# Start-up of a channel attention and gated feed-forward kernel: squares in PSUM, sums on two engines, eight units scored from high and low parts

## The chip, the cores and the metric

The kernel runs on one core of a Trainium2 chip. The metric is the device time of one execution in microseconds (us); before the change it is 2156.61 us, the median of three runs (2156.08 to 2156.77).

## What is computed

Four batches of q, k and v, each of 6080 rows and 256 channels in float32, go through an attention over channels, and its output through a feed-forward layer with the gate g = h * sigmoid(1.702 h):

```python
qn = q / (norm(q, axis=1) + 1e-6)
kn = k / (norm(k, axis=1) + 1e-6)
s = kn.T @ qn / tau            # 256 x 256 per batch
a = softmax(s - s.max(-1))     # divided by the sum + 1e-9
x = v @ a                      # 6080 x 256
h = x @ w_in                   # 256 -> 2048
out = (h * sigmoid(1.702 * h)) @ w_out
```

## The kernel before, in words

The rows of a batch lie on 128 partitions. Each partition holds 47 rows, and a tail of 64 rows is left. The work is cut into 25 units: units 0 to 22 have two row groups each (tiles of 128 x 512), units 23 and 24 have one (128 x 256). For one unit the scores take four products, of a 128 x 128 slice of k with 256 columns of q, in float32. The trace records each such float32 product as two matmuls (L348).

The first batch stands alone at the start, since nothing is there to overlap it with. `start_up` (L832) writes its order out by hand:

- SyncE loads q and k in tiles of up to six row groups, in order, into buffers of their own (L265, L269). GpSimd clears two tails (L268).
- For each unit, `prepare` (L279) squares q and k on ScalarE (L292) into one of three SBUF buffers. VectorE adds the two squares together, 1024 columns at once (L295), into one of two running sums. Even units go to one sum and odd units to the other.
- `score` (L365) of unit u - 7 is put behind `prepare` of unit u, on TensorE's queue. The scores collect in PSUM bank "o3". The first 18 units' scores are issued here, those of units 18 to 24 by the planner below.
- After the loads of the first batch, SyncE loads the first weights: `win_fetch` (L158, DMA at L120) into the buffers "qs" and "ks" of the pool `sp`, then `wout_fetch`, tau, `v_load` and the next batch's first rows.
- `add_both` (L298) adds the two sums and then the two halves (L300, L301). That finishes the sums of squares, called "acc" by the planner.

`first_softmax` (L852) and `together` (L1109) then lay out everything from the scores of unit 18 to the end of the first eight pairs of feed-forward blocks. They make a list of nodes with an engine, a duration and what they depend on. `arrange` (L1010) places them along a modelled time. The order on TensorE is fixed, except for the next batch's first scores, which are flexible fill. It is: scores of units 18, 19 and 20, the norms (`first_norms`, L449, matmul L453), scores 21 and 22, the spread of the norms (L480), scores 23 and 24, then the transposes of the softmax (L524). The model takes the time at which this stretch begins from START, that of the sums from `late_at(40.2, "acc")` (L869), and the first free times of ScalarE and VectorE from L1015. From the norms on, ScalarE takes their root (L460), VectorE turns it (L467 to L471), ScalarE makes a diagonal (L476), and so on to the softmax, while both engines also convert weights and split v.

After that the pairs follow (`lay`, L1537). There TensorE has matmuls of 512 columns on operands that are split into a high part (rounded to float32r) and a low part (the rest), with three products each. VectorE makes the low parts (L784 in the feed-forward, L312 for the scores of later batches) and GpSimd adds the squares of later batches (L332) and sums of v (L686).

The buffers that the change touches: the pool `sp` gives "qs" and "ks" two buffers each, the pool `vp` gives "pz_h" and "pz_l" two each. A buffer is given out again when its last reader is done. PSUM has eight banks of 512 float32: "a", "b", "c", "s" and "o0" to "o3".

Of the kernel before, what the change touches and what calls it, by code (L numbers as in the profile page):

```python
# [2 lines left out]

# [1 line left out]

# [6 lines left out]
F32 = mybir.dt.float32  # L12
F32R = mybir.dt.float32r
U32 = mybir.dt.uint32
AF = mybir.ActivationFunctionType
ALU = mybir.AluOpType
# [3 lines left out]
P = 128  # L20
# [3 lines left out]
NCH = 512  # L24
# [4 lines left out]
def channel_attention_then_glu(  # L29
# [23 lines left out]
    nc = tc.nc  # L53
    B, N, C = q.shape
# [7 lines left out]
    T = N // P  # L62
    TAIL = N - T * P
    UT = 2
    RT = 2
    SLOTS = 4
    WCH = 2 * NCH
    NCHUNK = -(-N // WCH)
    short = [NCHUNK - 2 if 0 < b < B - 1 else NCHUNK - 1 for b in range(B)]
    widths = [[WCH] * n + [N - (NCHUNK - 1) * WCH] + [WCH] * (NCHUNK - 1 - n) for n in short]  # L70
    chunks = [[(sum(w[:c]), w[c]) for c in range(NCHUNK)] for w in widths]
    STEPS = NF // 2 * SLOTS

    const = ctx.enter_context(tc.tile_pool(name="const", bufs=1))
    wp = ctx.enter_context(tc.tile_pool(name="wp", bufs=1))
    vp = ctx.enter_context(tc.tile_pool(name="vp", bufs=1))
    gp = ctx.enter_context(tc.tile_pool(name="gp", bufs=1))
    op = ctx.enter_context(tc.tile_pool(name="op", bufs=3))
    sp = ctx.enter_context(tc.tile_pool(name="sp", bufs=2))
    dram = ctx.enter_context(tc.tile_pool(name="dram", bufs=1, space=bass.MemoryType.DRAM))  # L80
    cv = ctx.enter_context(tc.tile_pool(name="cv", bufs=2))
# [5 lines left out]
    def bank(tag, name):  # L87
        pool = {"a": ps_h, "b": ps_h, "c": ps_h, "s": ps_s}.get(tag, ps_o)
        return pool.tile([P, NCH], F32, tag=tag, name=name)
# [65 lines left out]
    words = {}  # L155
    win = {}

    def win_fetch(n):  # L158


        g, c = divmod(n, NC2)
        gs = slice(2 * g * GW, 2 * (g + 1) * GW)
        src = w_in[c * P : (c + 1) * P, gs].rearrange("p (f w) -> p f w", w=2)
        if g == 0:
            room = (sp, ("qs", "ks")[c])
        else:
            room = (wp, f"{('wh', 'wl')[c]}{g}")
        words["in", n] = load_words(src, [P, GW], *room)
# [6 lines left out]
    def wout_fetch(u):  # L175

        rows = w_out[2 * u * P : 2 * (u + 1) * P, :]
        src = rows.rearrange("(f p) (d w) -> p f d w", p=P, w=2)
        words["out", u] = load_words(src, [P, 2, C])
# [19 lines left out]
    class Attention:  # L199
# [31 lines left out]

        def rooms(self, t0, room):
            n = (t0 + 4) // 6
            if t0 in (T - 3, T - 1):
                n = (t0 - T + 3) // 2
                tiles = [gp.tile([P, NCH], F32, tag=f"{t}{n}", name="raw") for t in ("gh", "gl")]
                return [t.rearrange("p (u c) -> p u c", u=UT) for t in tiles]
            if n in (4, 5):
                t = wp.tile([P, 2, NF // 2, C], F32, tag=("wo_h", "wo_l")[n - 4], name="raw")
                return [t[:, i] for i in range(2)]  # L240
            return [
                wp.tile([P, 6, C], F32, tag=f"{t}{n % 6}", name=f"raw_{s}")
                for t, s in (("wh", "q"), ("wl", "k"))
            ]

        def load(self, t0, room):

            b = self.b
            nt = min(room, T - t0)

            early = self.early.pop(0) if self.early else None
            cuts = (0, nt)
            if self.alone:
                tiles = self.rooms(t0, room)
                cuts = {2: (0, 2, 4, 6), 8: (0, 2, 6)}.get(t0, cuts)
            elif early:
                tiles = [
                    vp.tile([P, room, C], F32, tag=early + t, name="raw", bufs=2) for t in ("_h", "_l")
                ]
            else:  # L260
                tiles = [sp.tile([P, RT, C], F32, tag=t, name=t) for t in ("raw_q", "raw_k")]
            for a, z in zip(cuts, cuts[1:]):
                for src, t in zip((q, k), tiles):
                    body = src[b, : T * P, :].rearrange("(p t) c -> p t c", p=P)
                    nc.sync.dma_start(t[:, a:z, :], body[:, t0 + a : t0 + z, :])  # L265
                    if z == nt < room and TAIL:

                        nc.gpsimd.memset(t[TAIL:, nt, :], 0.0)  # L268
                        nc.sync.dma_start(t[:TAIL, nt, :], src[b, T * P :, :])  # L269
            for o in range(room):  # L270
                self.raw[t0 + o] = [t[:, o:, :] for t in tiles]
# [7 lines left out]
        def prepare(self, u):  # L279
            nt = self.units[u][1]  # L280
            if u == 0:
                self.sums_both = both = cv.tile([P, 2, UT, C], F32, tag="words", name="sums")
                *self.squares, self.sums_odd = [
                    vp.tile([P, 2, UT, C], F32, tag=tag, name="squares", bufs=2)
                    for tag in ("px_h", "px_l", "py_h", "py_l")
                ]
            elif u == 1:
                both = self.sums_odd
            else:
                both = self.squares[u % 3]  # L290
            for n, r in enumerate(self.fetched(u)):
                nc.scalar.activation(both[:, n, :nt, :], r, AF.Square)  # L292
            if u > 1:
                acc = (self.sums_both, self.sums_odd)[u % 2][:, :, :nt, :]
                nc.vector.tensor_tensor(acc, acc, both[:, :, :nt, :], op=ALU.add)  # L295
            return self.fetched(u)

        def add_both(self):  # L298
            acc = self.sums_both
            nc.vector.tensor_tensor(acc, acc, self.sums_odd, op=ALU.add)  # L300
            nc.vector.tensor_tensor(acc[:, :, 0, :], acc[:, :, 0, :], acc[:, :, 1, :], op=ALU.add)  # L301

        def part(self, u, n):
            nt = self.units[u][1]
            tag = ("qs", "ks")[n]
            self.parts[u, n] = t = sp.tile([P, UT, 2, C], F32R, tag=tag, name=tag)
            nc.scalar.copy(t[:, :nt, 0, :], self.fetched(u)[n])
# [57 lines left out]
        def score(self, u, qs, ks):  # L365
            nt = self.units[u][1]
            if u == 0:
                self.start_scores("o3")
            steps = [(j, i) for j in range(nt) for i in range(NC2)]
            last = u == len(self.units) - 1  # L370
            for j, i in steps:
                self.product(i, ks[:, j, i * P : (i + 1) * P], qs[:, j, :], last and j == nt - 1)

        def score_half(self, u):

# [440 lines left out]
    def keep_warm():  # L816

        wide = gp.tile([P, NCH], F32, tag="g", name="wide", bufs=2)
        nc.vector.memset(wide, 1.0)
        ps = bank("b", "ps_y")  # L820
        for rhs in [ones] * 4 + [wide]:
            nc.tensor.matmul(ps[:, : rhs.shape[1]], lhsT=ones, rhs=rhs, start=True, stop=True)  # L822

    nu = len(range(0, T, UT)) + (TAIL > 0)
    ats = [Attention(b, nu if b == 0 else 4 if b == 1 else 0) for b in range(B)]
    at, nxt = ats[:2]
# [5 lines left out]
    def start_up():  # L832
        nc.scalar.activation(table, ones[:, 0:1], AF.Sqrt)
        keep_warm()
        for u in range(nu):
            ready.append(at.prepare(u))
            if u >= AHEAD:
                at.score(u - AHEAD, *ready[u - AHEAD])
        win_fetch(0)
        win_fetch(1)  # L840
        wout_fetch(0)
        nc.sync.dma_start(tau_sb, tau.partition_broadcast(P))
        v_load(0, 0, False)
        v_load(0, 0, True)
        nxt.fetched(0)
        nxt.fetched(2)
        win_fetch(2)
        win_fetch(3)
        at.add_both()
        wo.extend(wp.tile([P, NF, C], F32R, tag=f"wo_{n}", name=f"wo_{n}") for n in "hl")  # L850

    def first_softmax():  # L852

        A = at
        us = 1.0 / 0.68
        START = 36.4

        def add(eng, dur, token, deps, fn, *a):
            gather[0].append(Node(eng, dur * us, token, deps, fn, a))

        def score(u, *deps):
            dur = 0.86 if u == nu - 1 else 1.72
            add("PE", dur, ("s", u), deps, lambda: at.score(u, *ready[u]))

        def late_at(t, *tokens):
            for token in tokens:
                done(token, (t - START) * us)

        late_at(40.2, "acc")  # L869
        late_at(34.7, ("cv", "in", 0, "load"))  # L870
        late_at(36.0, ("cv", "in", 1, "load"))
        late_at(37.3, ("cv", "out", 0, "load"))
# [137 lines left out]
    def arrange(nodes, row, ahead, near):  # L1010
# [1 line left out]
        ends = dict(begun_ends)  # L1012
        row = list(row)
        clock = dict.fromkeys(("PE", "ACT", "POOL", "SP"), 0.0)
        clock["ACT"], clock["DVE"] = 3.0, 5.6  # L1015
        open_to = {e: [] for e in clock}
        users = {}
        unmet = {}
# [39 lines left out]
        while undone:  # L1058
            best = None
            for e in clock:  # L1060
                at = list(choices(e))
                if not at:
                    continue
                t = min(r for r, _ in at)
# [13 lines left out]
            if best is None:  # L1078
                r, x = min((c for e in clock for c in choices(e)), key=lambda c: c[0])
                best = r, r, x  # L1080
            _, t, x = best
# [582 lines left out]
    for b in range(B):  # L1664
        for c in range(NCHUNK):
            if b or c:
                p = (b * NCHUNK + c) * PAIRS
                v_job(b, c, p - 1, p - 5)
        if b + 1 < B:
            o = b * NCHUNK * PAIRS  # L1670
            u, last_u = ats[b + 1].direct, len(ats[b + 1].units)
# [16 lines left out]
    with tc.manual_schedule():  # L1688
        start_up()
        together(PAIRS)  # L1690
        for p in range(PAIRS, TOTAL):
# [3 lines left out]
            t = now[0]  # L1695
# [33 lines left out]
```

## Time and profile before

| | |
|---|---|
| median of 3 runs | 2156.61 us |
| profiled execution: its own time | 2157.14 us |
| profiled execution: span from first to last instruction | 2155.4 us |
| TensorE busy | 2148.2 us |
| ScalarE busy | 1551.9 us |
| VectorE busy | 1288.2 us |
| GpSimd busy | 431.2 us |
| chain that ended last | TensorE 99% |

The profile is of one execution, whose own time is 0.5 us above the median. A timeline row gives the start, the duration, the engine (PE is TensorE, PEld its weight loads, DVE is VectorE, ACT is ScalarE, POOL is GpSimd, SPq the queue of SyncE), the source line, the operation, what is written from what is read, and the count. Instructions of one engine overlap a little at their ends, so the pace of a queue is the distance between starts, which is somewhat less than a duration.

### The profile page before, as it was taken

To read this page: it belongs to the slowest core of one execution; us is meant where nothing else is said; L and a number is where in the kernel's file an instruction comes from. 1 tells how busy PE (TensorE), PEld (TensorE's weight loads), DVE (VectorE), ACT (ScalarE), POOL (GpSimd) and SP (SyncE) were. 2 spreads that over 40 slices of the span, in tenths; PEclk is the share of its full clock that TensorE was granted. 3 is DMA by queue.
4 is the path that set the end of the run, shared out by engine and by line. 5 is a ranking of instruction groups with operands and counts; after the bars stand their busy time and mean duration, and the time that the engine had idled before them with its cause. 6 is when DMAs were issued, how large, how long until landed. Compare 5 with 4: busy or idle time off the path is not lost.

```text
span 2155.4 us, 26555 instructions
## 1 busy us (share of the span) xinstructions
PE 2148.2 (100%) x9720; PEld 1794.0 (83%) x9720; DVE 1288.2 (60%) x1925; ACT 1551.9 (72%) x2753; POOL 431.2 (20%) x457
## 2 busy tenths in 40 slices
PE   9999999999999999999999999999999999999999
PEld 8888888888888888888888888888888888888887
DVE  7986656665556665664555666566555545545543
ACT  7987777766777777776777777777676666666665
POOL 0003333230113342231012233223111200100100
PEclk9999999999999999999999999999999999999999
DMA  9433222221122222221113222122111110110100
GB/s 373 142 104 97 69 68 78 68 71 40 59 97 67 62 88 59 73 79 40 39 61 106 69 69 74 54 87 66 40 67 50 59 40 20 59 40 20 57 20 19
DMA packets 73843, 153.50 MB, mean 71 GB/s; under 512 B 6896, under 2 KB 14576, under 8 KB 73712
## 3 DMA queue, kind: packets, MB, share of 16 engines
q1 hardware_dynamic: 73712, 151.81, 21.3%
q8 instruction: 76, 1.25, 0.2%
q14 instruction: 55, 0.45, 0.1%
HBM read 122.68 MB, written 29.10 MB: 70 GB/s over the span
## 4 chain that ended last, share of the span: by engine, by line
PE 99%; ACT 1%; DMA 0%; issue 0%; DVE 0%; SPq 0%; ACTq 0%
PE ps_o L797 48%; PE ps_x L721 24%; PE ps_z L721 12%; PE ps_y L721 6%; PE s L387 4%; PE s L348 2%; PE ps_w L586 2%; PE ps_w L604 0%; DMA words<-in_w_in 0%; PE ps_y L822 0%; ACT vh L705 0%; PE ps_n L414 0%; ACT wf L621 0%; ACT eighths L136 0%; ACT z L134 0%
## 5 line engine op out<-in xcount | busy, mean ns | idle before, releaser
L797 PE MATMUL ps_o<-gh,wo_l 128*128 128x512 f32 (+1 forms) x1536 | 594.9, 387 | 0.0
L797 PE MATMUL ps_o<-gh,wo_h 128*128 128x512 f32 (+1 forms) x1536 | 594.8, 387 | 0.0
L797 PE MATMUL ps_o<-gl,wo_h 128*128 128x512 f32 (+1 forms) x1536 | 470.6, 387 | 0.0
L784 DVE TENSOR_TENSOR gl<-g,gh 128x512 fp32r<-128x512 f32 (+1 forms) x384 | 275.4, 756 | 155.7 <-ACT gh L780 155.7
L332 POOL TENSOR_TENSOR acc<-acc,sq 128x256 f32<-128x256 f32 x276 | 217.2, 793 | 600.5 <-ACT sq L320 589.7
L797 PEld LDWEIGHTS ps_o<-gh,wo_h 128*128 128x128 f32 x1536 | 288.3, 188 | 57.6
L797 PEld LDWEIGHTS ps_o<-gl,wo_h 128*128 128x128 f32 x1536 | 288.3, 188 | 57.5
L797 PEld LDWEIGHTS ps_o<-gh,wo_l 128*128 128x128 f32 x1536 | 288.3, 188 | 57.3
L784 DVE TENSOR_TENSOR gl<-ps_y,gh 128x512 fp32r<-128x512 f32 (+1 forms) x192 | 131.7, 686 | 339.0 <-ACT gh L780 338.6
L721 PE MATMUL ps_x<-vh,wh 128*128 128x512 f32 (+1 forms) x768 | 299.6, 390 | 0.6 <-ACT g L775 0.2
L721 PE MATMUL ps_x<-vl,wh 128*128 128x512 f32 (+1 forms) x768 | 298.0, 388 | 0.0
L721 PE MATMUL ps_x<-vh,wl 128*128 128x512 f32 (+1 forms) x768 | 297.5, 387 | 0.0
L686 POOL TENSOR_TENSOR v_raw<-v_raw 128x512 f32<-128x512 f32 (+1 forms) x110 | 167.8, 1534 | 515.6 <-DMA v_raw<-in_vT 433.7
L775 ACT ACTIVATE r<-r 128x512 f32<-128x512 f32 (+1 forms) x192 | 120.5, 628 | 170.1 <-DVE r L764 170.1
L755 ACT COPY r<-ps_x 128x512 f32<-128x512 f32 (+1 forms) x189 | 110.1, 583 | 168.8 <-PE ps_x L721 168.4
L780 ACT CAST gh<-g 128x512 fp32r<-128x512 f32 (+1 forms) x384 | 216.4, 613 | 0.1
L784 DVE TENSOR_TENSOR gl<-r,gh 128x512 fp32r<-128x512 f32 (+1 forms) x192 | 149.8, 780 | 61.6 <-ACT gh L780 58.4
L721 PEld LDWEIGHTS ps_x<-vh,wh 128*128 128x128 f32 x768 | 144.4, 188 | 29.3 <-ACT g L775 1.6
L721 PEld LDWEIGHTS ps_x<-vh,wl 128*128 128x128 f32 x768 | 144.2, 188 | 29.0
L721 PEld LDWEIGHTS ps_x<-vl,wh 128*128 128x128 f32 x768 | 144.5, 188 | 25.3
L755 ACT COPY r<-ps_z 128x512 f32<-128x512 f32 (+1 forms) x192 | 111.9, 583 | 71.6 <-PE ps_z L721 70.5
L405 DVE TENSOR_TENSOR sums<-sums,s 128x256 f32<-128x256 f32 x138 | 58.0, 420 | 160.2 <-PE s L387 157.8
(137 smaller groups left out, 3274.7 us busy)
## 6 DMA issues: line engine op xcount, KB each, us to landing
v_raw<-in_vT SPq DMA_DIRECT2D x80, 512.0 KB, 4.3
out_T<-osb SPq DMA_DIRECT2D x80, 256.0 KB, 2.0
raw_q<-in_q SPq DMA_DIRECT2D x74, 256.0 KB, 2.7
raw_k<-in_k SPq DMA_DIRECT2D x74, 256.0 KB, 2.7
win_h<-win_h SPq DMA_DIRECT2D x16, 512.0 KB, 3.3
win_l<-win_l SPq DMA_DIRECT2D x16, 512.0 KB, 4.2
v_raw<-in_vT SPq DMA_DIRECT2D x16, 480.0 KB, 3.8
words<-in_w_in SPq DMA_DIRECT2D x8, 512.0 KB, 5.2
```

The lines of the kernel that those rows point to most:

```text
L332: nc.gpsimd.tensor_tensor(acc, acc, sq[:, j, :], op=ALU.add)
L348: nc.tensor.matmul(self.s[:, i, :], lhsT=lhsT, rhs=rhs, start=self.first, stop=last, skip_group_check=True,)
L387: nc.tensor.matmul(out, lhsT=ks[:, j, low, ci], rhs=rhs, start=n == 0, stop=n == len(terms) - 1, skip_group_check=True,)
L405: nc.vector.tensor_tensor(out, out, part, op=ALU.add)
L586: nc.tensor.matmul(ps, lhsT=l[:, j, ci], rhs=r[:, j, :], start=n == 0, stop=n == 3 * NC2 - 1,)
L686: eng.tensor_tensor(out, a, z, op=ALU.subtract)
L721: nc.tensor.matmul(out, lhsT=l[:, wi, :], rhs=r[:, n, : self.hw], start=first and m == 0, stop=last and m == 2, skip_group_check=True,)
L755: nc.scalar.copy(r, getattr(self, src))
L775: nc.scalar.activation(g, source, AF.Gelu_apprx_sigmoid)
L780: nc.scalar.copy(gh, g)
L784: nc.vector.tensor_tensor(gl, g, gh.bitcast(F32), op=ALU.subtract)
L797: nc.tensor.matmul(out[d][:, : self.hw], lhsT=l[:, at_f, d * P : (d + 1) * P], rhs=r, start=first and l is wo[0] and r is gh, stop=last an ...
```

## The change

Squares of the first batch are written to six PSUM banks in turn, one for q and one for k of a unit, and VectorE adds each of them to a single running sum, 512 columns at a time. Units 4, 7, 10, 13 and 16 are left out of that: their squares go to SBUF, and GpSimd adds them to a second sum, which unit 1 began. VectorE joins the two sums behind unit 20's adds and folds the halves behind unit 22's. For units 6, 8, 10, ... 20 a new function, `split_unit`, copies q and k to their rounded high parts on ScalarE and subtracts these on VectorE for the low parts, just ahead of `prepare` of the unit after next. TensorE then scores such a unit by three products in place of one (high-high, high-low, low-high). The clearing of the tails goes from GpSimd to VectorE at the very start. The planner's figures are set anew.

```diff
+    LAST_ODD = 16
+    SPLIT = tuple(range(6, 21, 2))
...
         def prepare(self, u):
             nt = self.units[u][1]
             if u == 0:
...
+                self.rooms_ps = cycle(("a", "c", "o0", "o1", "o2", "b"))
+            odd = u % 3 == 1 and u <= LAST_ODD
+            acc = (self.sums_both, self.sums_odd)[odd]
             for n, r in enumerate(self.fetched(u)):
-                nc.scalar.activation(both[:, n, :nt, :], r, AF.Square)
-            if u > 1:
-                acc = (self.sums_both, self.sums_odd)[u % 2][:, :, :nt, :]
-                nc.vector.tensor_tensor(acc, acc, both[:, :, :nt, :], op=ALU.add)
+                if u < 2:
+                    out = acc[:, n]
+                elif odd:
+                    out = self.squares[u // 3 % 3][:, n]
+                else:
+                    out = bank(next(self.rooms_ps), "sq").rearrange("p (u c) -> p u c", u=UT)
+                out = out[:, :nt, :]
+                nc.scalar.activation(out, r, AF.Square)
+                if u > 1:
+                    eng = nc.gpsimd if odd else nc.vector
+                    eng.tensor_tensor(acc[:, n, :nt, :], acc[:, n, :nt, :], out, op=ALU.add)
             return self.fetched(u)

-        def add_both(self):
+        def add_odd(self):
             acc = self.sums_both
             nc.vector.tensor_tensor(acc, acc, self.sums_odd, op=ALU.add)
+
+        def add_halves(self):
+            acc = self.sums_both
             nc.vector.tensor_tensor(acc[:, :, 0, :], acc[:, :, 0, :], acc[:, :, 1, :], op=ALU.add)
+
+        def split_unit(self, u):
+            m = SPLIT.index(u)
+            for n, r in enumerate(self.fetched(u)):
+                pool, tag = (sp, ("qs", "ks")[n]) if m % 3 else (vp, ("pz_h", "pz_l")[n])
+                self.parts[u, n] = t = pool.tile([P, UT, 2, C], F32R, tag=tag, name=("qs", "ks")[n])
+                nc.scalar.copy(t[:, :, 0, :], r)
+                nc.vector.tensor_tensor(t[:, :, 1, :], r, t[:, :, 0, :].bitcast(F32), op=ALU.subtract)
...
             for j, i in steps:
-                self.product(i, ks[:, j, i * P : (i + 1) * P], qs[:, j, :], last and j == nt - 1)
+                ci = slice(i * P, (i + 1) * P)
+                if self.alone and u in SPLIT:
+                    qp, kp = self.parts[u, 0], self.parts[u, 1]
+                    for l, r in ((0, 0), (0, 1), (1, 0)):
+                        self.product(i, kp[:, j, l, ci], qp[:, j, r, :])
+                else:
+                    self.product(i, ks[:, j, ci], qs[:, j, :], last and j == nt - 1)
...
     def start_up():
...
+        at.tail_room()
         for u in range(nu):
+            if u - 2 in SPLIT:
+                at.split_unit(u - 2)
             ready.append(at.prepare(u))
+            if u == LAST_ODD + 4:
+                at.add_odd()
+            elif u == nu - 3:
+                at.add_halves()
             if u >= AHEAD:
                 at.score(u - AHEAD, *ready[u - AHEAD])
...
-        at.add_both()
...
+    START, ACC = 34.7, 39.2
...
-        START = 36.4
...
-            dur = 0.86 if u == nu - 1 else 1.72
+            dur = 0.86 if u >= nu - 2 else 1.44 if u in SPLIT else 1.72
...
-        late_at(40.2, "acc")
+        late_at(ACC, "acc")
...
-        clock["ACT"], clock["DVE"] = 3.0, 5.6
+        clock["ACT"], clock["DVE"] = (38.0 - START) / 0.68, (ACC - START) / 0.68
```

## Rows read from the trace of the kernel before

**Rows 1.** Busy time by stretch: us, PE, PEld, DVE, ACT, POOL, granted clock, DMA.

```profile
17.60:38.00 20.40, 20.40 (x96) 17.97 (x95) 18.41 (x16) 17.55 (x35) 0.00 (x0) 1.00 1.00 396
...
41.40:70.00 28.60, 26.95 (x130) 20.93 (x129) 28.27 (x65) 25.18 (x51) 0.00 (x0) 1.00 0.80 300
70.00:131.00 61.00, 61.00 (x302) 50.92 (x301) 60.10 (x123) 56.88 (x112) 0.00 (x0) 1.00 0.33 113
131.00:200.00 69.00, 68.70 (x305) 55.96 (x304) 45.50 (x68) 53.78 (x96) 14.68 (x18) 1.00 0.28 88
```

**Rows 2.** The chain that ended last, at the start-up: start, us, what.

```profile
6.92 34.77 PE s L348 x160
41.70 0.87 PE ps_n L453 x8
```

**Rows 3.** Timeline of PE: six products with split operands, and what follows them.

```profile
55.39 0.40 PE L604 MATMUL ps_w<-win_h,aT_h 128*128 128x256 f32 x2
55.63 0.40 PE L604 MATMUL ps_w<-win_l,aT_h 128*128 128x256 f32 x2
...
56.84 2.75 PE L348 MATMUL s<-raw 128*128 128x256 f32 x12
```

**Rows 4.** Timeline of ACT: squares of units 7 and 8, and the last ones.

```profile
17.14 0.63 ACT L292 ACTIVATE squares<-raw_k 128x512 f32<-128x512 f32 x1 [1.22 <-DMA raw_k<-in_k]
17.67 0.62 ACT L292 ACTIVATE squares<-raw_q 128x512 f32<-128x512 f32 x1
18.19 0.61 ACT L292 ACTIVATE squares<-raw_k 128x512 f32<-128x512 f32 x1
...
35.53 2.36 ACT L292 ACTIVATE squares<-raw 128x512 f32<-128x512 f32 x6
```

**Rows 5.** Timeline of DVE: sums of squares from unit 7 on, and what follows.

```profile
17.80 1.23 DVE L295 TENSOR_TENSOR squares<-squares 128x1024 f32<-128x1024 f32 x1 [1.31 <-ACT squares L292]
...
36.99 1.22 DVE L295 TENSOR_TENSOR sums<-sums,squares 128x1024 f32<-128x1024 f32 x1
38.13 0.68 DVE L295 TENSOR_TENSOR squares<-squares 128x512 f32<-128x512 f32 x1
38.73 0.68 DVE L295 TENSOR_TENSOR sums<-sums,squares 128x512 f32<-128x512 f32 x1
39.45 1.23 DVE L300 TENSOR_TENSOR sums<-sums,squares 128x1024 f32<-128x1024 f32 x1
40.71 0.69 DVE L301 TENSOR_TENSOR sums<-sums 128x512 f32<-128x512 f32 x1
...
45.08 0.14 DVE L467 RECIPROCAL rtau<-tau_sb 128x1 f32<-128x1 f32 x1
```

**Rows 6.** One line's instructions each: duration ns min/median/max, first and last start.

```profile
L760 ACT COPY ps_y<-ps_x x192: 543/570/607, 61.4 to 2137.6; 128x512 f32<-128x512 f32 x160, 128x480 f32<-128x480 f32 x32
...
L784 DVE TENSOR_TENSOR gl<-g,gh x384: 648/687/1789, 70.8 to 2146.4; 128x512 fp32r<-128x512 f32 x160, 128x480 fp32r<-128x480 f32 x32
...
L784 DVE TENSOR_TENSOR gl<-ps_y,gh x192: 648/692/693, 65.3 to 2141.4; 128x512 fp32r<-128x512 f32 x160, 128x480 fp32r<-128x480 f32 x32
...
L686 POOL TENSOR_TENSOR v_raw<-v_raw x110: 1212/1620/1787, 174.2 to 2045.7; 128x512 f32<-128x512 f32 x90, 128x480 f32<-128x480 f32 x20
```

**Rows 7.** Timelines of DVE and POOL where both work, around 200 us.

```profile
201.08 1.11 DVE L312 TENSOR_TENSOR ks<-raw_k,ks 128x512 fp32r<-128x512 f32 x1
215.25 2.55 DVE L784 TENSOR_TENSOR gl<-g,gh 128x512 fp32r<-128x512 f32 x2 [0.86 <-ACT gh L780]
237.06 1.30 DVE L784 TENSOR_TENSOR gl<-g,gh 128x512 fp32r<-128x512 f32 x2 [1.12 <-ACT gh L780]
...
200.07 1.56 POOL L332 TENSOR_TENSOR acc<-acc,sq 128x256 f32<-128x256 f32 x2 [2.19 <-ACT sq L320]
214.12 4.83 POOL L686 TENSOR_TENSOR v_raw<-v_raw 128x512 f32<-128x512 f32 x3 [0.87 <-DMA v_raw<-in_vT]
```

**Rows 8.** Timelines of SyncE and ACT: first weights issued, first wait for v.

```profile
30.98 2.20 SPq L120 DMA_DIRECT2D words<-in_w_in  x2
...
42.61 1.14 ACT L705 CAST vh<-v_raw 128x512 fp32r<-128x512 f32 x2 [2.00 <-DMA v_raw<-in_vT]
```

More of the change, by code (lines that the diff above doesn't have):

```diff
@@ L1 @@
 from contextlib import ExitStack
-from itertools import product
+from itertools import cycle, product
 import numpy as np
@@ L233, in rooms @@
             n = (t0 + 4) // 6
-            if t0 in (T - 3, T - 1):
+            if t0 == T - 1:
+                return self.tail
+            if t0 == T - 3:
                 n = (t0 - T + 3) // 2
@@ L244, in rooms, with tail_room @@
             ]
+        def tail_room(self):
+            tiles = [gp.tile([P, NCH], F32, tag=t, name="raw") for t in ("gh1", "gl1")]
+            self.tail = [t.rearrange("p (u c) -> p u c", u=UT) for t in tiles]
+            for t in self.tail:
+                nc.vector.memset(t[TAIL:, 1, :], 0.0)
         def load(self, t0, room):
@@ L266, in load @@
                     if z == nt < room and TAIL:
-                        nc.gpsimd.memset(t[TAIL:, nt, :], 0.0)
+                        if not self.alone:
+                            nc.gpsimd.memset(t[TAIL:, nt, :], 0.0)
                         nc.sync.dma_start(t[:TAIL, nt, :], src[b, T * P :, :])
@@ L281, in prepare @@
             if u == 0:
-                self.sums_both = both = cv.tile([P, 2, UT, C], F32, tag="words", name="sums")
+                self.sums_both = cv.tile([P, 2, UT, C], F32, tag="words", name="sums")
                 *self.squares, self.sums_odd = [
@@ L286, in prepare @@
                 ]
[L287 to L290, printed above, removed]
+                self.rooms_ps = cycle(("a", "c", "o0", "o1", "o2", "b"))
+            odd = u % 3 == 1 and u <= LAST_ODD
+            acc = (self.sums_both, self.sums_odd)[odd]
             for n, r in enumerate(self.fetched(u)):
-                nc.scalar.activation(both[:, n, :nt, :], r, AF.Square)
-            if u > 1:
-                acc = (self.sums_both, self.sums_odd)[u % 2][:, :, :nt, :]
-                nc.vector.tensor_tensor(acc, acc, both[:, :, :nt, :], op=ALU.add)
+                if u < 2:
[9 more added lines that the diff above has]
+                    eng.tensor_tensor(acc[:, n, :nt, :], acc[:, n, :nt, :], out, op=ALU.add)
             return self.fetched(u)
-        def add_both(self):
+        def add_odd(self):
             acc = self.sums_both
             nc.vector.tensor_tensor(acc, acc, self.sums_odd, op=ALU.add)
+        def add_halves(self):
+            acc = self.sums_both
             nc.vector.tensor_tensor(acc[:, :, 0, :], acc[:, :, 0, :], acc[:, :, 1, :], op=ALU.add)
+        def split_unit(self, u):
[5 more added lines that the diff above has]
+                nc.vector.tensor_tensor(t[:, :, 1, :], r, t[:, :, 0, :].bitcast(F32), op=ALU.subtract)
         def part(self, u, n):
```

## The prediction

> **What bounds the kernel now.** I read the busy times by stretch first, then the chain of waits, then each engine's timeline up to 60 us. From 70 us on TensorE is never idle and nothing there is edited, so only the start-up can move the time, and any delay made there stays [rows 1]. Up to 41.7 us the chain is TensorE alone: 160 matmuls of scores, units 1 to 20, without a gap, then the norms [rows 2]. One float32 record takes 34.77 / 160 = 0.217 us, a unit of eight 1.74 us. So unit 6 starts at 6.92 + 5 x 1.74 = 15.6 and unit 20 ends at 41.7. The other thing to see is how little room the neighbours have. ScalarE's last squares end at 37.9 [rows 4]; the sums of squares are done at 40.71 + 0.69 = 41.4 [rows 5], 0.3 us before the norms want them. From 41.4 to 131 us VectorE is busy for 88.4 of 89.6 us [rows 1], so it cannot catch up there.
>
> **TensorE's saving.** Twelve 256-column products with split operands take 56.84 - 55.39 = 1.45 us, weight loads included [rows 3]; a split unit needs just twelve. That is 0.29 less than 1.74, and 2.3 us for eight units, if operands are on time.
>
> **The first operands are late.** The copies of unit 6 are issued ahead of unit 8's squares, so behind unit 7's. The latter waits for its k until 17.14 [rows 4]; the pace of ScalarE is 18.19 - 17.67 = 0.52. So the copies start at 17.67 and 18.19, the second ends at 18.8, and VectorE's second subtraction (0.68) at 19.6. Now TensorE starts unit 6 at 15.6: it will stand still for about 4.0 us. That is more than the 2.3 saved. The loads that set 17.14 are not edited.
>
> **ScalarE.** Left from 17.67 on: 30 squares of 512 columns (units 8 to 22) at 0.52 = 15.6, four half squares at (2.36 - 2 x 0.52) / 4 = 0.33 [rows 4] = 1.3, and 16 copies at 0.52 = 8.3. Sum 25.2, so 42.9 where it was 37.9. No row has a square into PSUM; a copy from PSUM to PSUM has 0.57 for 0.62 [rows 4, 6], which would take 1.2 off for 24 squares, and I take the SBUF row, nothing else being known. Copies and squares cannot be hidden behind loads any more: after 17.6 ScalarE was busy for 17.6 of 20.4 us [rows 1], 2.8 free for 8.3.
>
> **VectorE.** Its pace is 1.14 for 1024 columns (38.13 - 36.99) and 0.60 for 512 (38.73 - 38.13) [rows 5]. From 18.3 on it has 24 adds of 512 (the twelve units from 8 to 22 that GpSimd does not take) = 14.4, 16 subtractions = 9.6, four adds of 256 at about 0.33 (0.60 less 256 columns at 0.54 per 512) = 1.3, the joining 1.14 and the folding 0.60. Sum 27.0, end 45.3. Some 1 us more goes where it waits for ScalarE, which has four operations where a split unit gives VectorE two: 46.4. An add from PSUM has a duration of 0.69 at most [rows 6], like one from SBUF; were 0.69 its pace too, 24 would cost 2.2 more, and I keep 0.60 as duration and form agree. GpSimd takes only four units off this stretch (7, 10, 13, 16), 4.6 us, while the splits bring 9.6. So without any clash the sums are ready at 46.4, 5.0 late.
>
> **The clash with GpSimd.** Ten adds of 512 on GpSimd at 1.2 to 1.8 us [rows 6] fill some 15 us of 11 to 33. In the rows where both work, a VectorE subtraction with two SBUF operands that starts at 201.08, in the middle of GpSimd's pair (200.07 to 201.63), takes 1.11 for 0.69, and ends 0.56 after the pair; two at 215.25 take 2.55, where the same two alone take 1.30 [rows 7]. The form with one PSUM operand never exceeds 693 ns, the one with two SBUF operands reaches 1789 [rows 6]. The squares in PSUM dodge this; the 16 subtractions do not. Those of units 8 to 16 fall among the adds of 10, 13 and 16. A pair that meets them costs 0.4 (one rest) to about 2 (a rest and a whole add), 1.25 in the row. Five pairs: 2 to 10, or nothing if they slip between. I take four at 1.25 = 5, as the row of the pair is the nearest. With them the sums come at 51.4, 10.0 late. The Trainium skill (SBUF — State Buffer, Who interferes with whom) has the same rule: a VectorE instruction with two SBUF inputs and a GpSimd one that reads SBUF exclude each other for a whole instruction. By it this trace's 1.11 and 2.55 are no accident, and a clash-free start-up should not be expected.
>
> **What waits behind.** With three units' banks in turn, ScalarE's square waits for VectorE's add of three units back, so ScalarE is held at VectorE's pace, at no extra cost. The buffers "qs" and "ks" have two rooms each; `win_fetch(0)` gets that of unit 16, so SyncE's load, issued at 30.98 [rows 8], now waits for score 16, near 43 in my sum, and tau, v and the next batch's rows queue behind it. The loads before it have drained by then, and the engines that want these words are as late, so I cost it at nothing; the cover is gone if SyncE is released later than 8 us ahead of the first use of v (42.61 before [rows 8]). add_odd's wait for GpSimd ends long before unit 20. Moved clearings of the tails: two short writes in an empty queue, nothing.
>
> **Sum.** Norms at 51.5 for 41.7: 9.8 late. VectorE continues its solid stretch 10 late. What can be given back is idle time of before: 1.65 us on TensorE and 0.33 on VectorE from 41.4 to 70, 0.9 on VectorE to 131 [rows 1]. I take 1.0. Delay 8.8. The profiled execution, 2157.14, would become 2165.9; the median lies 0.5 below it: 2165.4.
>
> **Rivals.**
> No clash: the subtractions slip between GpSimd's adds. Norms 4.8 late, less 1.0: 2160.4. For it: ScalarE feeds VectorE slowly and unevenly; against it, rows 7.
> Only the first stall: adds and copies are quicker than their rows and catch up by unit 20. 4.0 - 2.3 = 1.7 late: 2158.3. Against it, 27.0 us of work from 18.3 on.
> The other side: operands and sums are on time, and TensorE's saving decides: 2.3 less, 2154.3. It decides where unit 6's low part is there by 15.6 and the sums by 41.7 - 2.3 = 39.4. For it: TensorE is the only engine in the chain today. Against it: k of unit 7 lands at 17.1 and is ahead in ScalarE's queue.
> The clock: TensorE's granted clock is 1.00, the 2.4 GHz level, in all stretches [rows 1], where it hardly stood idle; idle times of 4 us at unit 6 and shorter ones after it are new. At 1.2 GHz a product takes twice as long. Up to the norms that is mostly hidden behind VectorE; if the clock is still low then, scores 21 to 24 (three units' work, 5.2 us) take 5 more: 2170.4. No row here shows the clock fall. The Trainium skill (TensorE: Matmul & The Clock Gate, the section on the HAM clock gate) says that idle time brings the half rate.
>
> **Numbers.** Forecast 0.60 (own range 2162 to 2170, clash 2 to 10 less what is given back), no clash 0.20, only the first stall 0.07, the gain 0.04, the clock 0.09. A measurement can tell about 0.2%, 4.3 us: the bounds are 2152.3 and 2160.9. Faster 0.02, as TensorE's whole saving falls short of 4.3. Same 0.19: the first stall, the rest of the gain and nearly half of no clash. Slower 0.79. The range 2159 to 2170.5 holds the forecast and no clash and leaves out the lowest two and the clock's upper end.
>
> **What would show it.** In the profile after: TensorE idle for some 4 us before unit 6 and again before later even units; VectorE solid from 18 to 50 us, its subtractions of units 8 to 16 at 1 to 2 us where GpSimd is busy, its adds from PSUM at 0.69; ScalarE's last squares near 47; the first w_in load issued after 37; norms near 51; the first 512-column matmuls of the pairs 9 us later than now. I am wrong if unit 6 starts before 17, or the norms before 45, or if the delay at the norms is gone by 131 us.

## The result and the profile after

The changed kernel takes 2169.72 us (median of six runs, 2169.11 to 2170.68) against 2156.69 for the kernel before, run beside it: 13.0 us more, a ratio of 1.006 with a 95% interval of 1.0047 to 1.0073. That is inside the predicted range and 4.3 above the predicted value. The profiled execution, whose own time of 2170.59 is 0.9 above the median, has a span of 2168.7 for 2155.4. Two executions of the record, one of the kernel before and one of the run without splits, took 3081 us at a mean granted clock of 0.65 and count in no median or ratio below.

TensorE's timeline shows most of it at a glance; the last bracket is the idle time ahead of an instruction and what ended it.

```profile
4.62 11.46 PE L376 MATMUL s<-raw_q,raw_k 128*128 128x256 f32 x48
18.93 0.39 PE L376 MATMUL s<-qs,ks 128*128 128x256 f32 x1 [2.85 <-ACT ks L328]
19.86 3.11 PE L376 MATMUL s<-qs,ks 128*128 128x256 f32 x11 [0.54 <-DVE qs L329]
...
26.23 1.46 PE L376 MATMUL s<-qs,ks 128*128 128x256 f32 x10 [1.02 <-DVE ks L329]
...
40.36 1.78 PE L376 MATMUL s<-qs,ks 128*128 128x256 f32 x12
...
43.51 1.78 PE L376 MATMUL s<-qs,ks 128*128 128x256 f32 x12
...
48.03 0.38 PE L376 MATMUL s<-qs,ks 128*128 128x256 f32 x1 [0.89 <-DVE qs L329]
48.63 1.45 PE L376 MATMUL s<-qs,ks 128*128 128x256 f32 x10 [0.22 <-DVE ks L329]
51.74 1.87 PE L487 MATMUL ps_n<-ones,sums 128*128 128x1 f32 x8 [1.65 <-DVE sums L312]
53.47 3.76 PE L376 MATMUL s<-raw_q,raw_k 128*128 128x256 f32 x8
57.02 2.15 PE L376 MATMUL s<-raw 128*128 128x256 f32 x8
```

The six units up to 16.08 run without a gap, as before. Unit 6 then waits 2.85 us for its high parts and 0.54 more for a low part. The later waits are for VectorE's low parts (ks, qs, L329) and at 51.74 for its sums. The same place in the trace of before, from the norms to unit 22:

```profile
41.55 1.02 PE L453 MATMUL ps_n<-ones,sums 128*128 128x1 f32 x8
42.43 1.97 PE L348 MATMUL s<-raw_q,raw_k 128*128 128x256 f32 x8
44.24 1.89 PE L348 MATMUL s<-raw 128*128 128x256 f32 x8
```

The norms come 10.0 us later than the 41.70 of [rows 2], or 10.2 from start to start in the two timelines. Then something else shows: the norms take 1.87 for 1.02, and unit 21's eight records 57.02 - 53.47 = 3.55 for 44.24 - 42.43 = 1.81. From the start of the norms to that of unit 22 it is 5.28 for 2.69, 2.6 us more. The busy times by stretch, TensorE alone, give the reason in the column of the granted clock (us, busy, clock, DMA share, GB/s):

```profile
18.00:20.00 2.00, 0.52 (x2) 0.99 1.01 421
20.00:22.00 2.00, 1.89 (x8) 0.50 1.04 433
...
50.00:52.00 2.00, 0.35 (x3) 0.68 0.92 343
52.00:54.00 2.00, 2.00 (x9) 0.50 1.06 411
54.00:56.00 2.00, 2.00 (x6) 0.50 1.05 416
56.00:58.00 2.00, 2.00 (x7) 0.62 1.02 411
```

After the waits ahead of unit 6, and from within the wait ahead of the norms, the clock is at 0.50, the 1.2 GHz level. The trace of before has 1.00 in every stretch of [rows 1].

VectorE's timeline, to be read beside [rows 5]: subtractions are L329 and adds L312. GpSimd's adds are the POOL rows of the second listing.

```profile
18.39 1.42 DVE L329 TENSOR_TENSOR qs<-raw_q,qs 128x512 fp32r<-128x512 f32 x1 [2.28 <-ACT qs L328]
19.73 0.68 DVE L329 TENSOR_TENSOR ks<-raw_k,ks 128x512 fp32r<-128x512 f32 x1
...
22.73 1.76 DVE L329 TENSOR_TENSOR qs<-raw_q,qs 128x512 fp32r<-128x512 f32 x1
24.41 1.76 DVE L329 TENSOR_TENSOR ks<-raw_k,ks 128x512 fp32r<-128x512 f32 x1
...
27.29 1.38 DVE L329 TENSOR_TENSOR qs<-raw,qs 128x512 fp32r<-128x512 f32 x1
28.59 1.76 DVE L329 TENSOR_TENSOR ks<-raw,ks 128x512 fp32r<-128x512 f32 x1
...
32.08 1.79 DVE L329 TENSOR_TENSOR ks<-raw,ks 128x512 fp32r<-128x512 f32 x1
33.79 2.47 DVE L312 TENSOR_TENSOR sums<-sums,sq 128x512 f32<-128x512 f32 x4
...
50.60 1.41 DVE L312 TENSOR_TENSOR sums<-sums,sq 128x256 f32<-128x256 f32 x4
...
61.45 0.48 DVE L528 SCALAR_TENSOR_TENSOR x<-s,rn,rq 128x256 f32<-128x256 f32 x1 [2.06 <-PE s L376]
```

```profile
17.99 1.26 POOL L312 TENSOR_TENSOR squares<-squares 128x512 f32<-128x512 f32 x1 [0.58 <-ACT squares L309]
22.67 2.95 POOL L312 TENSOR_TENSOR squares<-squares 128x512 f32<-128x512 f32 x2 [3.42 <-ACT squares L309]
26.83 2.97 POOL L312 TENSOR_TENSOR squares<-squares 128x512 f32<-128x512 f32 x2 [1.21 <-ACT squares L309]
32.04 2.98 POOL L312 TENSOR_TENSOR squares<-squares 128x512 f32<-128x512 f32 x2 [2.24 <-ACT squares L309]
```

VectorE goes from one instruction to the next from 18.4 to 52 us. Six of its sixteen subtractions take 1.38 to 1.79 where the others take 0.68, and all six lie where GpSimd adds: 5.8 us in sum. They are those of units 6 to 12. The adds from PSUM are not touched: four that start at 33.79, beside GpSimd's last pair, take 2.47, a pace of 0.60. At 61.45 VectorE has waited 2.06 us for TensorE, which is new: the last scores come late behind the slow norms and unit 21. In the run below that keeps TensorE busy, the wait is gone.

ScalarE's last square, and SyncE's first load of weights:

```profile
47.40 0.39 ACT L309 ACTIVATE sq<-raw 128x256 f32<-128x256 f32 x1 [0.21 <-DVE sums L312]
47.73 1.22 ACT L136 ACTIVATE z<-words 128x512 f32<-128x512 f32 x2
```

```profile
42.17 0.81 SPq L122 DMA_DIRECT2D words<-in_w_in  x2
```

The load waits for score 16 and is issued 11.2 later than in [rows 8], but the conversion that reads it, at 47.73, follows the squares without a wait.

### The profile page after: what moved, and what is told of

It is laid out like the page before. It is cut to its first block, busy times and chain, and to the rows that moved or that the text cites. A ratio compares the mean times of both kernels' runs of the same rounds, so it can differ in the third digit from the quotient of the medians.

```text
span 2168.7 us, 26700 instructions
## 1 busy us (share of the span) xinstructions
PE 2152.9 (99%) x9752; PEld 1797.9 (83%) x9752; DVE 1300.4 (60%) x1956; ACT 1560.6 (72%) x2769; POOL 443.2 (20%) x465
## 3 DMA queue, kind: packets, MB, share of 16 engines
q8 instruction: 76, 1.25, 0.3%
## 4 chain that ended last, share of the span: by engine, by line
PE 95%; DVE 2%; ACT 1%; issue 1%; DMA 1%; SPq 0%; DVEq 0%; ACTq 0%
PE ps_o L831 47%; PE ps_x L755 24%; PE ps_z L755 12%; PE ps_y L755 6%; PE s L421 4%; PE ps_w L620 2%; DMA raw_k<-in_k 1%; DVE sums L312 0%; PE s L376 0%; DVE ks L329 0%; PE ps_w L638 0%; ACT gh L814 0%; ACT g L809 0%; DVE vl L737 0%; ACT sq L309 0%
```

## The experiments

Each ratio is to the kernel before, run beside the experiment, with its 95% interval.

**No splits.**

```diff
-    SPLIT = tuple(range(6, 21, 2))
+    SPLIT = ()
```

START, the time of the sums, unit 23's duration and the first free times in the planner are set back to what they were before; these are the planner's old figures.

> The changed start-up with no split units (all scores in float32) and the planner's old figures; squares in PSUM and GpSimd's five units stay. Theory (the splits are what is too much): VectorE has 9.6 us less, the sums are ready near 41, unit 6 starts at 15.6, the norms at 41.7, time 2156.7 (2155.5 to 2157.7). Rival (the adds from PSUM or GpSimd's adds are a cost of their own): the sums come after 43 and the time is 2159 or more.

Measured: 2157.30 us, ratio 1.0001 (0.9991 to 1.0011). TensorE's norms, with no idle time from unit 1 on:

```profile
41.42 0.95 PE L487 MATMUL ps_n<-ones,sums 128*128 128x1 f32 x8
```

So squares in PSUM and GpSimd's adds cost nothing by themselves, and gain nothing. Without subtractions beside them GpSimd's pairs run at their own pace:

```profile
20.02 2.51 POOL L312 TENSOR_TENSOR squares<-squares 128x512 f32<-128x512 f32 x2 [1.33 <-ACT squares L309]
```

The whole loss goes with the split units and the planner's new figures, which this run lacks too; the figures are tried alone below.

**Nothing on GpSimd.** The splits stay.

```diff
-            odd = u % 3 == 1 and u <= LAST_ODD
+            odd = u == 1
```

> The changed kernel with units 4, 7, 10, 13 and 16 on VectorE too, from PSUM; nothing on GpSimd. Theory (the clash costs more than GpSimd takes over): VectorE has eight adds of 0.60 more from 18 us on, 4.8 us, but all subtractions take 0.68; norms near 49.2 for 51.7, time 2167.2 (2165.5 to 2168.5). Rival (the clash is small, the load decides): norms at 54 to 56.5, time 2172 to 2174.

Measured: 2167.66 us, ratio 1.0048 (1.0033 to 1.0063). VectorE's first subtractions, and then the norms on TensorE:

```profile
18.50 0.68 DVE L329 TENSOR_TENSOR qs<-raw_q,qs 128x512 fp32r<-128x512 f32 x1
19.10 0.68 DVE L329 TENSOR_TENSOR ks<-raw_k,ks 128x512 fp32r<-128x512 f32 x1
```

```profile
49.57 1.86 PE L487 MATMUL ps_n<-ones,sums 128*128 128x1 f32 x8 [1.66 <-DVE sums L312]
```

All sixteen subtractions take 0.68 or 0.69. With more work on VectorE the norms come 2.2 us earlier. GpSimd's help costs more than it takes over: 5.8 us of lengthened subtractions for six adds, 3.6 us. Of the eight adds that had been counted, those of unit 7 come ahead of the first subtraction, at 18.50. The norms and unit 21 are slow here too (1.86, and 3.50 to the start of unit 22).

**TensorE kept busy.** Matmuls of ones into the bank "s", which nothing uses yet.

```diff
+    def fill(n):
+        for _ in range(n):
+            nc.tensor.matmul(at.spare, lhsT=ones, rhs=at.wide, start=True, stop=True)
+
+    FILL = {6: 4, 8: 1, 10: 1, 20: 1}
...
+        at.spare = bank("s", "spare")
...
+                fill(FILL.get(u - AHEAD, 0))
                 at.score(u - AHEAD, *ready[u - AHEAD])
...
-            add("PE", dur, ("s", u), deps, lambda: at.score(u, *ready[u]))
+            add("PE", dur, ("s", u), deps, lambda: (fill(FILL.get(u, 0)), at.score(u, *ready[u])))
...
-        add("PE", 0.65, "ns", ["acc"], A.first_norms)
+        add("PE", 0.65, "ns", ["acc"], lambda: (fill(2), A.first_norms()))
```

> The changed kernel with matmuls of ones into a spare bank where TensorE stood idle: four before unit 6, one before units 8, 10 and 20, two before the norms. Theory (the half clock after the norms' wait is 2.8 us of the loss): granted clock 1.00 up to 60 us, norms in 0.9 and unit 21 in 1.74 us, first pair's products 2.8 us earlier, time 2166.9 (2165.8 to 2168). Rival (VectorE is as late anyway): clock up, norms shorter, but the first pair's products where they were, time 2169.7 (2168.7 to 2170.7).

Measured: 2167.48 us, ratio 1.0046 (1.0031 to 1.0061); beside the changed kernel's 2169.72 that is 2.2 less, and 2.6 less if each is counted from the kernel before run beside it (10.4 more for 13.0). The two intervals overlap, so the evidence is the trace. TensorE at the norms and units 21 and 22, and the mean clock of two stretches:

```profile
51.55 1.05 PE L487 MATMUL ps_n<-ones,sums 128*128 128x1 f32 x8
52.47 1.97 PE L376 MATMUL s<-raw_q,raw_k 128*128 128x256 f32 x8
54.28 1.89 PE L376 MATMUL s<-raw 128*128 128x256 f32 x8
```

```profile
16.00:24.00 8.00, 7.23 (x30) 1.00 1.02 428
...
52.00:60.00 8.00, 7.34 (x36) 1.00 1.04 419
```

The norms start 0.2 us earlier than without the filling, unit 22 starts 2.7 us earlier (54.28 for 57.02), and the first products of the pairs start at 67.70 for 70.70. So the half clock at unit 6 was hidden behind VectorE, and the one at the norms was not.

**Both together:** the edits of the last two in one kernel.

> No units on GpSimd and, in the same kernel, the matmuls of ones that keep TensorE busy. Theory (clash and half clock add up): norms at 49.5, clock 1.00, time 2165.4 (2164.3 to 2166.5). Rival (both hide behind the same wait): 2167 or more.

Measured: 2165.44 us, ratio 1.0038 (1.0024 to 1.0052), the norms at 49.61 in 1.05. The two parts add up: 2.1 and 2.2 alone, 4.3 together, or 2.4, 2.6 and 4.5 if each is counted from the kernel before run beside it.

**The planner's old figures** on the changed kernel, with the splits.

> The changed kernel with the planner's old figures (START 36.4, 40.2 for the sums, old first free times), so another order after the norms. Theory (the order behind the norms is not the cause): norms at 51.7 as before, time 2169.7 give or take 1.2. Rival (an order made for sums at 39.2 costs on top of the delay): 2167 or less.

Measured: 2168.84 us, ratio 1.0053 (1.0038 to 1.0068), norms at 51.62. A gain of 0.9 against the changed kernel can't be told from none. Its trace shows where such a gain could come from:

```profile
51.62 1.05 PE L487 MATMUL ps_n<-ones,sums 128*128 128x1 f32 x8 [1.65 <-DVE sums L312]
52.53 3.46 PE L376 MATMUL s<-raw_q,raw_k 128*128 128x256 f32 x8
55.79 2.13 PE L376 MATMUL s<-raw 128*128 128x256 f32 x8
```

The waits are those of the changed kernel (0.89, 0.22 and 1.65), yet here the norms run at full speed and only unit 21 is slow: unit 22 starts at 55.79 for 57.02. So the same waits cost 1.5 us here and 2.6 there. The order behind the norms is no large part.

**No low parts.** The 16 subtractions are left out; all twelve products of a split unit read the high parts, so the rest of q and k of eight units is missing in the scores.

```diff
-                nc.vector.tensor_tensor(t[:, :, 1, :], r, t[:, :, 0, :].bitcast(F32), op=ALU.subtract)
...
-                        self.product(i, kp[:, j, l, ci], qp[:, j, r, :])
+                        self.product(i, kp[:, j, 0, ci], qp[:, j, 0, :])
```

> The changed kernel without the low parts: the 16 subtractions are left out, and the twelve products of a split unit all read the high parts, so the scores are those of the rounded values. Theory (the subtractions, by their load of 9.6 and the clash, make most of the delay; ScalarE's copies a smaller part): ScalarE's last squares near 42.9, norms at 44.9 (44 to 46), time 2160.5 (2158.5 to 2162.5). Rival (the copies on ScalarE are the bound): norms at 48 or later, time 2164 or more.

Measured: 2165.34 us, ratio 1.0037 (1.0024 to 1.005): the time misses what was expected by some 5, though the norms are where they should be. TensorE, and ScalarE at the end of its squares:

```profile
18.64 1.70 PE L375 MATMUL s<-qs,ks 128*128 128x256 f32 x12 [2.37 <-ACT ks L328]
...
45.02 1.87 PE L486 MATMUL ps_n<-ones,sums 128*128 128x1 f32 x8 [2.56 <-DVE sums L312]
46.74 3.76 PE L375 MATMUL s<-raw_q,raw_k 128*128 128x256 f32 x8
```

```profile
40.35 2.34 ACT L309 ACTIVATE sq<-raw 128x512 f32<-128x512 f32 x6
```

ScalarE ends at 42.69, where the copies alone were reckoned to put it (42.9), and the norms at 45.02 are 3.3 late. So the subtractions with their clash make 6.7 of the 10.0 us at the norms, and stall and copies the rest. What had been left out of the expectation is the wait of 2.56 ahead of the norms, after which norms and unit 21 run at half clock again (1.87, 3.56). That is 2.6 us: unit 22 starts at 50.30, 6.1 late. The median is 8.4 above the kernel before, so some 2 us have no run that tells where they are from. The profiled execution shows 1.1 of it, as its span is 7.2 longer. The planner's new figures, which this kernel has, were not taken out.

**One split unit.**

```diff
-    SPLIT = tuple(range(6, 21, 2))
+    SPLIT = (6,)
```

The planner has its old figures.

> The changed start-up with unit 6 alone split, the planner's old figures. Theory (the first operands are late whatever the load): TensorE stands still for some 3 to 4 us before unit 6, then at half clock for 2 to 3 us; the sums are ready by 41 as without splits, the norms come near 46 (45 to 47.5), time 2161 (2159.5 to 2163). Rival (the stall is made good later, as VectorE and ScalarE are on time and work ahead): norms near 46 but time within 1.5 of the kernel before.

Measured: 2162.36 us, ratio 1.0025 (1.0015 to 1.0035). TensorE ahead of unit 6, and the norms:

```profile
18.51 0.58 PE L376 MATMUL s<-qs,ks 128*128 128x256 f32 x1 [2.79 <-ACT ks L328]
19.45 3.10 PE L376 MATMUL s<-qs,ks 128*128 128x256 f32 x11 [0.35 <-DVE qs L329]
...
47.79 0.95 PE L487 MATMUL ps_n<-ones,sums 128*128 128x1 f32 x8
```

One unit, split too early, costs 5.4 us: over 3 us of waiting and a stretch at half clock from 19.5 on. Behind the norms TensorE's idle time up to 170 us is 1.0 for 2.0 before, so no more than about 1 us is made good. The norms, at 47.79, are 6.1 late and 0.3 beyond the range that was expected, though VectorE has its sums at 41.5 as before, since here nothing hides the slow matmuls.

**A version that might have gained:** no splits, GpSimd takes units 4 and 7 alone (LAST_ODD = 7), old figures.

> A version that might beat the kernel before: no split units, squares in PSUM, GpSimd takes units 4 and 7 alone, the planner's old figures. VectorE is free at 39.7 for 41.3, TensorE's part is as before. Theory (TensorE is the bound up to the norms, VectorE after them): up to 1.5 us less, 2155.8 (2155.0 to 2156.8). Rival (nothing is waiting for VectorE there): 2156.9.

Measured: 2156.72 us, ratio 1.0 (0.999 to 1.0009). VectorE is free 1.0 us earlier than before (40.28 for 41.32; 39.7 had been expected), and nothing comes of it. The chain of waits there goes over a load, not over VectorE:

```profile
34.72 7.31 DMA v_raw<-in_vT
...
42.05 1.14 ACT vh L739 x2
43.19 0.07 ACT rn L494
```

ScalarE's root of the norms stands behind the high parts of v in its queue, and these wait for v. No version found here beats the kernel before.

## Why the prediction was right, and where it was off

- Unit 6's wait, 4.0 predicted from 15.6 on: 2.85 + 0.54 from 16.08 on. TensorE began with the high parts alone before the low parts were there, which the step had not allowed for. The run with one split unit shows it to be a loss by itself. The step was right.
- VectorE's load and the clash: sums at 51.4 predicted, 52.0 measured; the clash 5 predicted (four pairs at 1.25), 5.8 measured (six subtractions in four pairs); the pace of adds from PSUM 0.60, as taken. The runs without low parts and without GpSimd bear out both parts. The step was right in mechanism and in size, but the pairs that clash are those of units 6 to 12, not of units 8 to 16, so that four pairs came out is partly luck. GpSimd took three units off this stretch and not the four that were counted (7, 10, 13, 16), as the run without it shows for unit 7. The Trainium skill's rule (SBUF — State Buffer, Who interferes with whom) is borne out: two-input subtractions are held, PSUM adds are not, and GpSimd is held as well (2.95 for 2.51 a pair).
- ScalarE at VectorE's pace, last squares near 47: 47.8. SyncE's load near 43: 42.17, at no cost that the trace of the changed kernel shows. In the run that keeps TensorE busy, TensorE waits 0.66 us at 58.99 for the next batch's k, which is queued behind that load. Both steps were right.
- Norms at 51.5: 51.74.
- The clock was put down as a rival with a chance of 0.09, at 5 us more. It came: the trace puts 2.6 us on it, and the run that keeps TensorE busy 2.2 to 2.6. The step that failed is the sum's silence after the norms: it carried 9.8 on at full clock, where the norms and unit 21 ran at 0.50. The Trainium skill's rule cited with it (TensorE: Matmul & The Clock Gate, the section on the HAM clock gate) is that idle time brings the half rate. These traces agree in the main: the clock is at 0.50 after TensorE stood idle, and at 1.00 again in 58 to 60 us.
- "1.0 given back" was mis-sized: nothing was. Unit 22 starts 12.8 late (57.02 for 44.24), which is 10.2 at the norms and 2.6 of half clock; the span is 13.3 longer. From the norms to 170 us TensorE is idle for 2.1 us, and for 2.0 before. The pairs' first products come 11.5 late (70.70 for 59.24, where 9 was predicted), only because eight fewer records of the next batch's scores lie ahead of them. After 143 us TensorE's idle time is 0.2 us in 2007 in both traces, so the loss is made before that and stays. The prediction's "never idle" from 70 us on is 0.3 us too strong by its own rows (68.70 of 69.00).
- TensorE's saving is there: a split unit and the float32 unit behind it take 43.51 - 40.36 = 3.15 together, so a split unit takes 1.41 beside 1.74, where 1.45 was predicted. Waits ate it.

The forecast 2165.4, plus the 2.6 of the clock, the 1.0 not given back and the 0.4 by which the norms are later than forecast (10.2 for 9.8), is 2169.4, for 2169.72 measured.

## What to carry to other kernels

A saving on the busiest engine is worth nothing if its neighbours must make the operands and have no room; count their work from the point where it can start, in the order in which it is queued, and look first at the first operand. Here, moving adds to GpSimd cost more than it took over while VectorE had instructions that read two SBUF operands, and gained nothing where it had none, so look at what VectorE does meanwhile. A wait on TensorE can cost twice, once as idle time and once as a stretch at half clock behind it; a few matmuls of ones into a spare bank, put where it waits, show whether it does.

## What was not expected of the hardware

The clock fell after short waits: ahead of the norms TensorE stood idle for 0.89, 0.22 and 1.65 us, the products of unit 20 between them, and the mean clock of 50 to 52 us is 0.68, so it fell before the last of these waits was over. A wait of 2.37 ahead of unit 6, in the run without low parts, did not bring it down: the clock is 1.00 from 18 to 22 us there. And with the planner's old figures the same three waits left the norms at full speed and slowed unit 21 alone, so the length of a wait did not settle what it cost.

GpSimd's add of two 128x512 float32 tiles takes 1.25 us a piece here, not the 1.54 that the 90 sums of v of that shape show on average before. The 79 of these that overlap a VectorE instruction with two SBUF operands have a median of 1.62, and the other 11 take 1.28 to 1.30, which fits the clash seen above.
